# Moving weight conversions, normalising steps, folds and feature sums between the slots of a hand-planned mLSTM, Fourier and MLP kernel

## The chip, the core and the metric

The kernel runs on one core of a Trainium2 chip. The metric is the device time of one execution in microseconds (us); the time of a kernel is the median of its runs. Five engines work side by side, each through its own queue in order: TensorE (PE, with its weight loads as PEld), VectorE (DVE), ScalarE (ACT), GpSimd (POOL) and SyncE (SP), which here issues the DMAs. [...]

## The reference

Batch 4, 8 heads, 768 tokens, 40 features a head, all in float32. An mLSTM cell runs over the tokens of each head:

```python
m_new = np.maximum(f_gate[t] + m, i_gate[t])
f_stab, i_stab = np.exp(f_gate[t] + m - m_new), np.exp(i_gate[t] - m_new)
C = f_stab * C + i_stab * outer(v[t], k[t])        # 40 x 40 state
n = f_stab * n + i_stab * k[t]
y[t] = sigmoid(o_gate[t]) * (C @ q[t]) / max(abs(n @ q[t]), 1)
```

The eight heads of a token side by side are its 320 features x. Over them goes a Fourier mix and an MLP:

```python
u = x + real(fft(fft(x, axis=tokens), axis=features))
un = (u - mean(u)) / sqrt(var(u) + 1e-6)
out = u + relu(un @ w_ch1) @ w_ch2                 # 320 -> 1280 -> 320
```

## The kernel before

**A planner written out by hand.** Nothing is issued where it is defined. `at(slot, phase, fn, ...)` puts a step down, and `run` issues all steps in the order of (slot, phase). The phases are `EVAC` 0, `FILL` 1, `MAIN` 2, `FILL_PE` 3, with fractions between. A slot is about one step of the MLP on TensorE, which stands at `MAIN`; what stands at `FILL` comes before it on each queue, what stands at `FILL_PE` after it. Slot and phase thus set the order on each engine's queue and nothing else. Two steps that share no engine may change places without effect.

**The mLSTM.** Each batch's tokens are cut into six chunks c of 128. Batch 0 has a plan of its own; batches b of 1 to 3 go through `plan_halves`, three slots a chunk, beside the MLP of the batch before. For chunk (b, c), beginning in slot s:

- `mlstm_exp` (L491, ACT), `mlstm_scale_q` (L501, POOL) and `mlstm_mask` (L515, POOL) prepare weights and queries.
- `halves_scores` and `halves_to_state` (PE, `ps<-qk` and `ps<-vw`) write the scores' bank, which exists once. `halves_weigh` (L672, DVE) and two `halves_add` (L667, DVE, the state adds) read it, and free it for the next chunk.
- The heads: `halves_from_state` and the first `halves_from_chunk` (PE, `ph<-C,qg` and `ph<-kvt,W`), then `halves_between`, an ACT copy of one element (L699, `warm`) for which the second `halves_from_chunk` waits. Their bank exists once too.
- `mlstm_finish` (L712 to L720, five DVE instructions, the finish (b, c)) normalises and gates out of the heads' bank, and so frees it for the next chunk's heads. `halves_rows` (SP, some POOL) moves rows of chunks 0, 1, 2 and 3.

**The mix.** `mix_fold` (L812 to L828, mostly DVE) folds a pair of chunks for the transform; `mix_seq`, `mix_tail` and `mix_feat` (PE, `pz`, `pzt`, `pu`) transform; `mix_add` (L957 to L963, six DVE instructions, the addition of chunk c) adds the result and takes mean and variance; `mix_center` (L971), `mix_turn` and `mix_turn_out` (L983) turn the chunk. `mix_rstd` and three `mix_rstd_step` (L1002 to L1005, POOL) give the deviation by Newton steps.

**The MLP.** Batch 0's (slots 31 to 62) is plain: `mlp_in` (L1056 and L1047), `mlp_relu` (L1071), `mlp_out` (L1181), `residual` (L1187, DVE). Batches 1, 2 and 3 (32 slots each from 63, 95 and 127) save products by sums: `mlp_sums` (L1106, DVE, the feature sums) before the first block; five blocks of four slots (L1118, and L1123 for the tails), whose partial results DVE adds (L1127, one add in a block's second slot and three in its third); then three pairs of four slots each (L1237), each with two banks that TensorE overwrites in the next slot once DVE's residual (L1187) has read them, and `hidden_sums` (L1223, DVE).

**Weight conversions.** The MLP's weights come as 64-bit floats. Ten pieces are each loaded (SP, `raw`, two buffers), taken apart (`take`, L406 and L408, DVE), converted (`convert`, L413 and L414, ACT) and put together (`join`, L420, L422 and L426, DVE). Those of `w_ch2` are done beside batch 0's MLP; the list `when` holds slot and phase of each. Matmul results rotate over four banks given out by `bank`, and the mix of batches 2 and 3 has banks of its own choice among them.

Of the kernel before, what the change touches and what calls it, by code (L numbers as in the profile page):

```python
# [20 lines left out]
NT = S // L  # L21
# [9 lines left out]
TG = NT // 2  # L31
# [22 lines left out]
def kernel(  # L54
# [69 lines left out]
    def at(slot, phase, fn, *args):  # L124
        plan.setdefault((slot, phase), []).append((fn, args))
# [7 lines left out]
    EVAC, FILL, MAIN, FILL_PE = range(4)  # L133
# [628 lines left out]
    def plan_halves(b, s0, stride=3):  # L762
        for c in range(NT):
            s = s0 + stride * c
            t = 22 + 2 * c if b == 1 and c < 3 else s - 5
            at(t, FILL, mlstm_load, b, c)
            at(t, FILL, mlstm_load_max, b, c)
            at(34 if b == 1 and c == 2 else t + 1, FILL, mlstm_load_decay, b, c)
            at(s - 1, FILL, mlstm_load_o, b, c)
            at(s - 1, FILL, mlstm_scale_v, b, c)  # L770
            at(s - 1, FILL + 0.3, mlstm_exp, b, c, 0)
            at(s, FILL, mlstm_exp, b, c, NP)
            at(s, FILL_PE + 2.05, halves_scores, b, c)
            at(s, FILL_PE + 2.5, halves_to_state, b, c)
            for i in range(2):
                at(s + i, FILL + 0.05, halves_decay, b, c, i)
                at(s + 1 + i, FILL - 0.2, halves_add, b, c, i)
            at(s, FILL + 0.1, mlstm_scale_q, b, c)
            at(s + 1, FILL, mlstm_mask, b, c)
            at(s + 1, FILL + 0.55 if b == 1 and c > 0 else MAIN + 0.7, halves_weigh, b, c)  # L780
            end = c == NT - 1
            at(s + 3, MAIN - 0.1 if end else FILL_PE, halves_from_state, b, c)
            at(s + 3, MAIN - 0.1 if end else FILL_PE, halves_from_chunk, b, c, 0)
            at(s + 3, MAIN if end else FILL_PE + 0.5, halves_between, b, c)
            at(s + 3, FILL_PE + 3, halves_from_chunk, b, c, 1)
            at(s + 3, FILL_PE + 0.6, mlstm_tanh, b, c)
            at(s + (5 if (b, c) == (2, 2) else 4), FILL + 0.3 if b == 1 else MAIN + 0.55, mlstm_finish, b, c)
            at(s + 6, FILL - 0.6, halves_rows, b, c)

# [215 lines left out]
    def plan_mix(b, s0, x_done, s_feat, s_add, s_turn):  # L1007
        for j in range(TG):
            p = TG - 1 - j
            at(x_done[j] + (b > 1 and j == TG - 1), FILL + 0.5 if b < 2 else FILL_PE + 0.2, mix_fold, b, p)  # L1010
            if b == 0:
                at((s0 - 4, s0 - 2, s0)[j], FILL_PE + 4, mix_seq, b, p, (0, 1))
                at((s0 - 2, s0 - 2, s0)[j], FILL_PE + 4, mix_tail, b, p)
            elif b == 1 or j == 0:
                if b > 1:
                    for step, slot in enumerate((x_done[0], x_done[-1] + 2, x_done[-1] + 6)):
                        at(slot, FILL_PE + 0.25, mix_fold_again, b, step)
                at(s0, FILL_PE + 4, mix_seq, b, p, (0,))
                at(s0 + 1, FILL_PE + 4, mix_seq, b, p, (1,))
                at(s0 + 2, FILL_PE + 4, mix_tail, b, p)  # L1020
        for i in range(2):
            at(s0 + 1 if b == 0 else s0 + 1 + i, FILL, mix_seq_out, b, i)
        at(s0 + (1 if b == 0 else 3), FILL + 0.1, mix_tail_out, b)
        for p in range(TG):
            at(s_feat[p], FILL_PE + 4, mix_feat, b, p)
        for c, a, t in zip(ORDER, s_add, s_turn):
            at(a, FILL if b < 2 else MAIN + 0.5, mix_add, b, c)
            at(t, FILL + 0.1, mix_center, b, c)
            at(t, FILL_PE + (5 if b == 0 or c in ORDER[:4] else -0.1), mix_turn, b, c)
            if b > 0:  # L1030
                at(t, FILL_PE + 6, mix_turn_out, b, c)
            elif t < s_mlp:
                at(t + 1, FILL + 0.2, mix_turn_out, b, c)
            else:
                at(t + 1, EVAC, mix_turn_out, b, c)
# [232 lines left out]
    def plan_mlp(b, s):  # L1268
        groups = range(NT // TG)
        for i in range(NFF // 2) if b > 0 else ():  # L1270
            for step in range(4):
                at(s, MAIN, mlp_block, b, i, step)
                s += 1
            end = i == NFF // 2 - 1
            for n, (gr, f) in enumerate(((1, 2 * i + 1), (1, 2 * i), (0, 2 * i))):
                at(*((s - 1, MAIN + (-0.1 if gr else 0.1)) if end else (s + n, MAIN + 0.5)), mlp_relu_in_place, gr, f)
        for gr in groups if b == 0 else ():
            for f in range(NFF):
                at(s, MAIN, mlp_in, b, gr, f)
                s += 1  # L1280
                if f % 2:
                    at(s, EVAC, mlp_relu, b, gr, f - 1)
                    at(s, EVAC, mlp_relu, b, gr, f)
        if b > 0:
            for j in range(1, 5):
                at(s - (5, 4, 3, 3)[j - 1], FILL_PE + 0.3, hidden_sums, 0, (j,), 0, NFF // 2 - 2)
            at(s, EVAC, hidden_sums, 0, (1, 2), NFF // 2 - 2, NFF // 2)
            at(s, MAIN + 0.1, hidden_sums, 0, (3, 4), NFF // 2 - 2, NFF // 2)
        for n in range(TG) if b > 0 else ():
            for step in range(4):  # L1290
                at(s, MAIN, mlp_out_pair, b, n, step)
                if n < TG - 1 and step > 1:
                    for j in (2 * step - 3, 2 * step - 2):
                        at(s, MAIN + 0.6, hidden_sums, n + 1, (j,))
                s += 1
        for gr in groups if b == 0 else ():
            for i in range(TG):
                for half in range(2):
                    at(s, MAIN, mlp_out, b, gr, i, half)
                    s += 1  # L1300
                at(s, EVAC, mlp_store, b, gr, i)
# [5 lines left out]

    def plan_batch(b, s_mlstm, s_mix, s_mlp):
        (plan_halves if b > 0 else plan_mlstm)(b, s_mlstm)
        done = [s_mlstm + n for n in ((16, 19, 22) if b == 0 else (18, 21, 22))]  # L1310
        assert s_mix >= done[-1] and s_mlp >= s_mix + 9
        late = [s_mlp + 2 * c for c in range(TG)]
        if b == 0:
            feat = [s_mix + 1, s_mix + 1, s_mlp + 3]
            turn = [s_mix + 2, s_mix + 3, s_mix + 4]
            add = turn + [s_mlp, s_mlp + 4, s_mlp + 5]
            late = [s_mlp + 2, s_mlp + 5, s_mlp + 7]
        else:
            feat = [s_mix + c for c in ((3, 4, 6) if b == 1 else (3, 4, 7))]
            add = [s_mix + c for c in ((4, 4, 5, 6, 7, 7) if b == 1 else (4, 5, 5, 6, 8, 9))]  # L1320
            turn = [s_mix + c for c in ((5, 6, 6) if b == 1 else (6, 7, 8))]
            late = [s_mix + c for c in ((7, 8, 8) if b == 1 else (9, 10, 10))]
            at(s_mlp, EVAC + 0.5, mlp_sums)
        plan_mix(b, s_mix, done, feat, add, turn + late)
        s = s_mlp + NFF + 2
        at(s, FILL + 0.6, mix_rstd, b)
        for n in range(3):
            at(s + 3 * n if b == 0 else s, FILL + 0.65, mix_rstd_step, b)
        plan_mlp(b, s_mlp)

    s_mlp = 31
    plan_batch(0, 0, 22, s_mlp)
    plan_batch(1, 32, 54, s_mlp + MLP_SLOTS)
    plan_batch(2, 53, 83, s_mlp + 2 * MLP_SLOTS)
    plan_batch(3, 83, 115, s_mlp + 3 * MLP_SLOTS)
    for n in range(4):
# [4 lines left out]

    when = [((2, 0.7), (4, 0.5), (6, 0.6)), ((6, 0.7), (7, 0.5), (8, 0.6)), ((11, 0.7), (13, 0.5), (22, 0.6))]
    when += [((22, 0.7), (23, 0.7), (27, 0.6)), ((27, 0.7), (28, 0.7), (32, 0.6))]
    when += [((33, 0.7), (34, 0.3), (34, 0.6)), ((34, 0.7), (35, 2.7), (36, 0.6))]
    when += [((s, 0.7), (s + 1, 0.7), (s + 2, 0.6)) for s in (36, 39, 42)]
    pieces = w1_pieces + w2_pieces
    for n, (w, p) in enumerate(zip(when, pieces)):
        if n > 4:
# [138 lines left out]
```

## Time and profile before

| | |
|---|---|
| median of 14 runs | 402.73 us (401.38 to 403.95) |
| the profiled execution | 402.7 us, its span 401.0 us |
| TensorE busy | 382.9 us, 95% of the span |
| VectorE, ScalarE, GpSimd busy | 279.7, 171.8, 133.0 us |
| mean granted TensorE clock | 0.991 of full speed |
| DMA | 44.78 MB, 112 GB/s in the mean |

Times in the text that name no duration are microseconds from the span's start. In the timeline a row has the start, the length, engine, line, operation, tiles, shapes and count; in brackets the idle time of the engine before it and what ended that. Ends of matmuls are modelled, and pipelined matmuls start a little before their predecessor's end.

### The profile page before, as it was taken

How to read it: one execution, taken by the hardware profiler on the slowest of the kernel's cores; microseconds unless marked ns; L12 is line 12 of the kernel's file. 1: busy time of each engine (PE TensorE's matmuls, PEld its weight loads, DVE VectorE, ACT ScalarE, POOL GpSimd, SP SyncE). 2: the span in 40 equal slices, each digit the busy share in tenths (PEclk: the TensorE clock that was granted, in tenths of full speed). 3: DMA queues.
4: the chain of work that ended last, by engine and by line, in shares of the span. 5: the costliest groups of instructions: out<-in, count | busy, mean ns of one | idle time of the engine just before them, and what ended most of it. 6: DMA issues, size and time to landing. Idle time of an engine off the chain costs nothing.

```text
span 401.0 us, 10588 instructions
## 1 busy us (share of the span) xinstructions
PE 382.9 (95%) x4174; PEld 278.7 (69%) x4174; DVE 279.7 (70%) x671; ACT 171.8 (43%) x481; POOL 133.0 (33%) x237
## 2 busy tenths in 40 slices
PE   8999899979999999998999989989999999999996
PEld 6877555545567677755569888845578987556996
DVE  7789988999766467485775498777764686336652
ACT  6887367655640232655463214544440023454000
POOL 5648512555763341253255124451310000020000
PEclk9999999979999999999999999999999999999999
DMA  7988499777276244356800526410000000000000
GB/s 215 292 244 238 139 246 272 192 196 221 68 188 170 61 154 129 120 129 177 194 1 28 141 67 207 133 38 2 0 0 18 17 34 33 2 0 0 34 33 34
DMA packets 25631, 44.78 MB, mean 112 GB/s; under 512 B 5727, under 2 KB 14766, under 8 KB 25454
## 3 DMA queue, kind: packets, MB, share of 16 engines
q1 hardware_dynamic: 25582, 44.11, 38.4%
q8 instruction: 33, 0.54, 0.6%
q14 instruction: 16, 0.13, 0.1%
HBM read 38.49 MB, written 4.12 MB: 106 GB/s over the span
## 4 chain that ended last, share of the span: by engine, by line
PE 67%; DVE 22%; issue 5%; DMA 3%; ACT 2%; POOL 0%; SPq 0%; DVEq 0%; POOLq 0%
PE po L1237 18%; PE pm L1118 14%; PE po L1181 8%; PE pm L1056 5%; PE ph L519 4%; PE pm L1123 4%; PE ps L519 2%; PE pu L935 2%; DVE so L716 2%; DVE h L1127 2%; DMA qk<-in_qkT 1%; PE pz L892 1%; PE put L978 1%; DVE x L720 1%; PE pm L1047 1%
## 5 line engine op out<-in xcount | busy, mean ns | idle before, releaser
L1187 DVE SCALAR_TENSOR_TENSOR x<-po,rstd,x 128x160 f32<-128x160 f32 (+1 forms) x69 | 26.9, 394 | 43.7 <-PE po L1237 36.8
L1127 DVE TENSOR_TENSOR h<-h,pm 128x384 f32<-128x384 f32 x60 | 30.5, 549 | 29.2 <-PE pm L1123 13.9
L652 POOL TENSOR_TENSOR C<-C,decB 128x164 f32<-128x164 f32 x30 | 15.9, 531 | 75.8 <-DVE C L667 66.4
L1118 PE MATMUL pm<-uT,w_sb 128*128 128x384 f32 x90 | 37.8, 507 | 2.0 <-DVE h L1127 1.3
L491 ACT ACTIVATE W<-W,colT 128x64 f32<-128x64 f32 x144 | 37.3, 339 | 0.0
L1181 PE MATMUL po<-w_sb,h 128*128 128x320 f32 x120 | 34.2, 435 | 0.0
L515 POOL TENSOR_SCALAR_AFFINE_SELECT W<-W 64x512 f32<-64x512 f32 x36 | 27.5, 764 | 12.3 <-ACT W L491 11.1
L1056 PE MATMUL pm<-uT,w_sb 128*128 128x384 f32 x80 | 31.2, 528 | 0.3 <-DVE x L955 0.2
L1002 POOL TENSOR_TENSOR t<-rstd 128x6 f32<-128x6 f32 x12 | 3.4, 282 | 81.9 <-DVE v L996 81.3
L1237 PE MATMUL po<-T,S 128*128 128x160 f32 x180 | 27.9, 302 | 1.5 <-DVE x L1187 1.5
L501 POOL TENSOR_TENSOR qg<-qk,Gb 128x512 f32<-128x512 f32 (+1 forms) x21 | 28.8, 1370 | 0.8 <-DMA Gb<-G_d 0.7
L1181 PEld LDWEIGHTS po<-w_sb,h 128*128 128x128 f32 x120 | 22.3, 190 | 9.4 <-issue 0.6
L1237 PEld LDWEIGHTS po<-T,S 128*128 128x128 f32 x180 | 25.5, 190 | 3.2 <-DVE x L1187 2.0
L1118 PEld LDWEIGHTS pm<-uT,w_sb 128*128 128x128 f32 x90 | 15.5, 189 | 16.3 <-DVE h L1127 7.5
L1237 PE MATMUL po<-w_sb,h 128*128 128x160 f32 x180 | 26.3, 300 | 0.0
L1237 PEld LDWEIGHTS po<-w_sb,h 128*128 128x128 f32 x180 | 25.2, 190 | 1.4 <-DVE x L1187 0.3
L1174 ACT ACTIVATE h<-h 128x384 f32<-128x384 f32 x45 | 23.1, 520 | 2.0 <-DVE h L1127 2.0
L1123 PE MATMUL pm<-uT,w1t_sb 64*128 64x384 f32 x120 | 23.4, 509 | 0.0
L983 ACT COPY uT<-put 128x384 f32<-128x384 f32 x24 | 11.1, 476 | 27.5 <-PE put L978 27.5
L1056 PEld LDWEIGHTS pm<-uT,w_sb 128*128 128x128 f32 x80 | 15.1, 202 | 11.0 <-issue 3.2
L971 ACT ACTIVATE uc<-x 128x384 f32<-128x384 f32 x24 | 14.4, 613 | 18.3 <-DVE x L963 12.2
L507 POOL TENSOR_TENSOR vw<-kvt,colT 128x328 f32<-128x328 f32 x23 | 17.8, 772 | 12.8 <-DVE colT L360 10.1
(241 smaller groups left out, 843.6 us busy)
## 6 DMA issues: line engine op xcount, KB each, us to landing
kvt<-in_kv SPq DMA_DIRECT2D x24, 336.0 KB
qk<-in_qkT SPq DMA_DIRECT2D x48, 160.0 KB
raw<-in_w SPq DMA_DIRECT2D x10, 640.0 KB
Gb<-G_d SPq DMA_DIRECT2D x36, 128.0 KB
W<-M_d SPq DMA_DIRECT2D x36, 128.0 KB
so<-in_o SPq DMA_DIRECT2D x24, 160.0 KB
out<-x SPq DMA_DIRECT2D x24, 160.0 KB
x<-so SPq DMA_DIRECT2D x9, 140.0 KB
```

The costliest lines, as they stand in the source:

```text
L491: nc.scalar.activation(out=k.W[:, h, :], in_=M, func=AF.Exp, scale=-1.0, bias=colT[:, c, 0, b * H + h:b * H + h + 1])
L501: nc.gpsimd.tensor_tensor(out=k.qg[:, :, t], in0=k.qk[:, 0, :, t], in1=k.Gb[:, :, t], op=OP.mult)
L515: nc.gpsimd.affine_select(out=W, in_=W, compare_op=OP.is_ge, fill=0.0, base=base, pattern=[[0, H], [step, LH]], channel_multiplier=-1)
L519: nc.tensor.matmul(out, w, x, start=start, stop=True, skip_group_check=True)
L1056: nc.tensor.matmul(k.pm[i], w1_sb[:, ch, f0:f0 + L], u[2 * ch], start=(ch == 0 and not ahead), stop=(ch == 1 and ahead), skip_group_check= ...
L1118: nc.tensor.matmul(bank, w, u, start=start, stop=True, skip_group_check=True)
L1123: nc.tensor.matmul(bank, block(w1t_sb, i)[rows], mlp_u(gr, 1)[rows], start=False, stop=True, skip_group_check=True)
L1127: nc.vector.tensor_tensor(out=h, in0=h, in1=bank, op=OP.add)
L1174: nc.scalar.activation(out=h, in_=h, func=AF.Relu, scale=-1.0)
L1181: nc.tensor.matmul(k.po, hidden(gr, f)[:, i * L:(i + 1) * L], w2_sb[:, f, :], start=(f == 0), stop=(f == NFF - 1))
L1187: nc.vector.scalar_tensor_tensor(out=u, in0=po, scalar=k.rstd[:, c:c + 1], in1=u, op0=OP.mult, op1=OP.add)
L1237: nc.tensor.matmul(po, a[:, f], w[:, f], start=start and f == 0, stop=f == half - 1, skip_group_check=True)
```

## The change

No instruction is added or taken away; steps get another slot or phase.

- Weight pieces 6 to 9 (counted from 0): the convert goes behind the slot's state adds and exponentials, the join one slot later or at the slot's head, and take and load of pieces 7 to 9 a slot later.
- Folds of batch 1: from slots 50, 53 and 54 to 49, 50 and 52.
- Finishes: (2,5) two slots later; (3,0) and (3,2) one slot later; (2,4), (3,3) and (3,4) in their slot, but ahead of the MLP step's adds.
- Heads of (2,5): in their slot 71, but behind the MLP step and no longer ahead of it.
- `halves_rows` is not called for chunks 4 and 5, for which it does nothing.
- Batches 2 and 3: the addition of chunk 5 goes one slot earlier, into the slot of chunk 0's (87 and 119).
- Feature sums of batches 2 and 3: from the head of the first block's slot to the end of the slot before.

```diff
-            end = c == NT - 1
+            end = c == NT - 1 and b != 2
...
-            at(s + (5 if (b, c) == (2, 2) else 4), FILL + 0.3 if b == 1 else MAIN + 0.55, mlstm_finish, b, c)
-            at(s + 6, FILL - 0.6, halves_rows, b, c)
+            at(s + ((4, 4, 4, 4, 4, 4), (4, 4, 5, 4, 4, 6), (5, 4, 5, 4, 4, 4))[b - 1][c],
+               FILL + 0.3 if b == 1 or (b, c) in ((2, 4), (3, 3), (3, 4)) else MAIN + 0.55, mlstm_finish, b, c)
+            if c < TG + 1:
+                at(s + 6, FILL - 0.6, halves_rows, b, c)
...
-        done = [s_mlstm + n for n in ((16, 19, 22) if b == 0 else (18, 21, 22))]
+        done = [s_mlstm + n for n in ((16, 19, 22), (17, 18, 20), (18, 21, 22), (18, 21, 22))[b]]
...
-            add = [s_mix + c for c in ((4, 4, 5, 6, 7, 7) if b == 1 else (4, 5, 5, 6, 8, 9))]
+            add = [s_mix + c for c in ((4, 4, 5, 6, 7, 7) if b == 1 else (4, 4, 5, 6, 8, 9))]
...
-            at(s_mlp, EVAC + 0.5, mlp_sums)
+            at(*((s_mlp, EVAC + 0.5) if b == 1 else (s_mlp - 1, MAIN + 0.7)), mlp_sums)
...
-    when += [((33, 0.7), (34, 0.3), (34, 0.6)), ((34, 0.7), (35, 2.7), (36, 0.6))]
-    when += [((s, 0.7), (s + 1, 0.7), (s + 2, 0.6)) for s in (36, 39, 42)]
+    when += [((33, 0.7), (34, 0.3), (34, 0.6)), ((34, 0.7), (36, 0.7), (37, 0.3))]
+    when += [((s, 0.7), (s + 2, 0.7), (s + 3, 0.3)) for s in (37, 40, 43)]
```

## Prediction

> **What bounds the kernel now.** I read the page first, then TensorE's own waits, then the sums by stretch and the timeline around each wait.
>
> ```profile
> span 401.0 us, 10588 instructions
> ...
> PE 382.9 (95%) x4174; PEld 278.7 (69%) x4174; DVE 279.7 (70%) x671; ACT 171.8 (43%) x481; POOL 133.0 (33%) x237
> ```
>
> Who TensorE waited for (us in total, times, longest us):
>
> ```profile
> PE po L1237 <- DVE x L1187: 2.5, 3, 1.1
> PE ps L519 <- DVE C L667: 1.9, 1, 1.9
> PE ph L519 <- ACT warm L699: 1.4, 2, 1.1
> PE pm L1118 <- DVE h L1127: 1.3, 2, 1.0
> ...
> PE ph L519 <- DVE x L720: 1.0, 1, 1.0
> ```
>
> The sums by stretch (length, then busy PE, PEld, DVE, ACT, POOL, then granted clock, DMA share, GB/s):
>
> ```profile
> 82.00:87.00 5.00, 1.99 (x95) 1.65 (x86) 4.70 (x6) 3.33 (x9) 2.93 (x3) 0.77 0.71 212
> 87.00:91.50 4.50, 4.50 (x13) 2.72 (x10) 3.88 (x10) 2.19 (x7) 2.82 (x4) 0.50 0.89 252
> 91.50:95.00 3.50, 3.50 (x13) 1.55 (x11) 3.24 (x5) 3.13 (x8) 2.27 (x2) 1.00 0.94 280
> ```
>
> TensorE is the bound: it idles 401.0 - 382.9 = 18.1 us. Since the change leaves its work alone, only these waits can move, plus one stretch at half clock: the last rows show 0.77, then 0.50, then 1.00. The timeline (start, length, what, wait before it) shows why:
>
> ```profile
> 77.68 2.82 PE L1056 MATMUL pm<-uT,w_sb 128*128 128x384 f32 x8 [0.16 <-DVE x L955]
> ...
> 80.42 0.81 DVE L420 SCALAR_TENSOR_TENSOR e<-raw,e 128x640 uint32<-128x640 uint32 x1
> ...
> 83.39 0.83 ACT L413 ACTIVATE e<-e,ebias 128x640 uint32<-128x640 uint32 x1 [3.65 <-DVE e L406]
> 83.67 0.32 DVE L667 TENSOR_TENSOR C<-C,ps 128x164 f32<-128x164 f32 x1
> 84.04 0.69 PE L519 MATMUL ps<-qk 40*64 40x64 f32 x32 [1.86 <-DVE C L667]
> ...
> 86.40 0.67 PE L519 MATMUL ph<-kvt,W 64*64 64x41 f32 x16 [1.15 <-ACT warm L699]
> ...
> 87.69 4.63 PE L1056 MATMUL pm<-uT,w_sb 128*128 128x384 f32 x8
> ...
> 201.81 0.91 PE L1118 MATMUL pm<-uT,w_sb 128*128 128x384 f32 x2 [0.22 <-DVE h L1127]
> ```
>
> A weight join (L420) and take stand ahead of the short state add (L667) that frees the scores' bank; on ACT the convert (L413), waiting for that take, stands ahead of the copy (L699) that TensorE waits for next. Then eight passes take 4.63 us instead of 2.82.
>
> **Weight conversions.** The join and the next take go behind the second state add, the convert behind the exponentials and the copy. Gone: 1.86 + 1.15 = 3.0 us of waits; 0.4 of pipelining, since a successor otherwise starts about 0.2 us before its predecessor's modelled end; 4.63 - 2.82 = 1.8 at half clock; and 0.35 on the transposes behind (0.90 instead of 0.55 at 76.97). Sum 5.6.
>
> Next late: the last join moves to slot 46. It fits DVE's 2.74 us wait before the state add at 112.18 if it runs like the join at 80.42 (0.81 + 0.81 + 0.83 = 2.5), not if like the one at 84.25 beside POOL (to 88.2, 4.0). The finish of chunk 4 follows, and the next heads start at 114.99, only 0.4 us after its end at 114.61. Cost 0 to 1.6; I take 0.5, nearer the first join, since only one large POOL step (L501, 111.14 to 112.42) lies there. First part: -5.1. On ACT one convert now lies ahead of the copy L983 at 77.55 and delays it by 0.75 us; it frees a bank at 78.8 that the third matmul of the 77.68 group, two pairs of passes on, wants at 79.0. Nothing, or up to 0.75 if that cover goes. On SP, raw loads stand behind row moves instead of ahead; raw is loaded two slots ahead and the one wait for it on DVE was 1.64 at 67.61, behind which nothing of TensorE was late. Nothing.
>
> **Feature sums, rows, folds of batch 1.** `mlp_sums` keeps its neighbours on every queue except for the finish dealt with below, and rows of chunks 4 and 5 issue nothing: both free. The folds (1.7 us each) and POOL's third Newton step move before the first residual at 123.66, for which DVE waited 2.79. Free; without that cover one residual is 0.5 late, against four rotating banks.
>
> **Finishes (2,4), (2,5) and the heads behind the block.** Finish (2,4) (1.65 us, 187.10 to 188.75) runs in the 2.49 us that DVE waits before 185.70; the 1.02 at 188.89 goes. Heads (2,5) lose their cover: a block's pair of passes lay between their first half and the half that waits for the ACT copy. Now the pair comes first (187.7), the first half at 188.35 for 0.95, the copy 0.1 behind it for 0.13, the second half from 189.6 for 0.4: slot 72 starts at 190.0 instead of 190.99. But finish (2,5), 1.65 us now placed in a 1.72 us wait, goes to slot 74, into a stretch without a gap: from the end of slot 73's adds (196.19) to those of slot 77 (201.22) DVE works 5.0 us; then 6.7, from 1.0 earlier, so the adds come at 201.9 and TensorE restarts 0.6 later than today: its wait there grows from 0.22 to 1.8. Bounds -1.0 (DVE catches up) to +1.0. I take +0.6.
>
> **Two additions share slot 87, finish (3,0) to slot 88.** The addition (1.74 us) and the finish (1.71) change places ahead of the residual that TensorE waits 1.08 for at 234.88: no change. But the finish then ends at 238.4, and the heads at 237.80 need its bank: a wait of 0.75 (with the 0.14 that followed L720 at 188.75), in front of all that TensorE has queued, of which 0.44 is recovered at 247.28, where TensorE waits for DVE anyway. +0.3 (0 to 0.8).
>
> **Finish (3,2) to slot 94, (3,3) ahead of an add.** (3,2) would start at the residual after 257.35 and end at 259.4 (today 257.39). Heads at 258.57 wait 1.0; the feature sums start at 259.3 instead of 258.44. Finish (3,3) (1.65) delays the add at 263.24, whose bank the tails then overwrite. The wait of 1.04 at 266.70 takes some of that in. Bounds: 0 (today's sums, 4.2 us beside POOL, run like those at 336.87, 2.3) to 0.9; I take +0.5.
>
> [...]
>
> **Batch 3, same pair of additions in slot 119.** Today both stand in slot 120, and TensorE waits 1.01 at 321.55. One goes ahead of a residual that frees a bank at 317.33: new wait 0.5, old one gone. -0.6 (-1.0 to 0).
>
> **Sum.** -5.1 + 0.6 + 0.3 + 0.5 - 0.6 = -4.3. The profiled execution took 402.7 us (span 401.0 and 1.7 around it), the runs' median being 402.73: 398.4 us.
>
> **Rivals.** (a) The half clock stays in the first MLP for another reason: 1.8 + 0.35 less, 400.6. Against: nowhere else did it fall, and it fell inside the stretch with the only wait above 1.3. [...]
>
> (b) Slower: the half clock moves to the new waits. It lasted from about 84.7 (the 0.77 above) to 91.5, 6.8 us; among dense matmuls that costs 3.4. New places: the 1.8 us at 200.6 to 202.4, and the 1.0 before the small heads at 258.57. One gives 401.8, two give 405.2; two decide. For: 1.8 is the size that did it. Against: four waits of 1.0 to 1.1 (188.89, 234.88, 266.70, 321.55) cost no clock, and matmuls around 201 are dense.
>
> (c) Transfers become the bound of the first MLP. From 82 to 95 they moved 5 x 212 + 4.5 x 252 + 3.5 x 280 thousand bytes, 3.2 MB; in 13 - 5.6 = 7.4 us that is 430 GB/s, against 292 in the best slice. At that rate they take 10.9 us and come 3.5 late, less their lead in the buffers (0 to half): 400.1 to 401.9. Against: the 10 us behind them moved only 68 GB/s.
>
> **Chances.** Forecast 0.60, (a) 0.12, (b) once 0.10, twice 0.05, (c) 0.10, below the range 0.03. The range goes down by two thirds of what all small terms at their lower ends would give (0.5 + 1.6 + 0.3 + 0.5 + 0.4 = 3.3), to 396.2, and up to 401.2, which takes in (a) and most of (c). About 0.2% (0.8 us) can be told from no change: faster 0.87 (all but part of (b), with 401.8 on the edge), same 0.05, slower 0.08.
>
> **What would show it.** Right: no wait at `ps<-qk` and `warm` near 82 to 87, clock 1.00 there, the second x8 group at 2.8; a wait near 1.8 on L1127 in the fourth block of batch 1; waits on L720 at the heads of (3,1) and (3,3); none at the T4 product of batch 3's second pair. Wrong: a half clock anywhere, or waits for DMA or L667 in slots 41 to 50.

## The result: 407.86 us, 1.3% slower, and the profile after

The median after is 407.86 us (10 runs, 406.49 to 408.76), against 402.49 for the kernel before on the same chip. The ratio is 1.0135, with a 95% interval of 1.0119 to 1.0150: 5.4 us slower, where 4.3 us faster was forecast. The profiled execution took 408.68 us, 5.98 more than the one before. From the page after, the span and the busy times:

```profile
span 406.9 us, 10596 instructions
...
PE 387.4 (95%) x4174; PEld 280.8 (69%) x4174; DVE 280.9 (69%) x671; ACT 171.9 (42%) x481; POOL 133.8 (33%) x237
```

TensorE idles 406.9 - 387.4 = 19.5 us, only 1.4 more than before. Its busy time grew by 4.5 us for the same 4174 matmuls: it ran slower for longer, at a mean granted clock of 0.983 instead of 0.991. Who TensorE waited for (us in total, times, longest us):

```profile
PE ph L519 <- DVE x L720: 3.4, 3, 1.7
PE pm L1125 <- DVE h L1129: 2.1, 2, 1.7
PE ph L519 <- DVE so L720: 1.6, 2, 0.8
PE po L1239 <- DVE x L1189: 1.3, 2, 1.1
```

The waits of 1.86 and 1.15 us in the first block are gone, as forecast. In their place stand waits for the last instruction of the finishes (L720) and one of 1.7 us before the tails (L1125). The sums by stretch of the kernel after (columns as in the prediction; the granted clock is the third number from the end):

```profile
82.00:95.00 13.00, 13.00 (x192) 7.55 (x183) 12.51 (x21) 8.17 (x21) 9.64 (x11) 1.00 0.88 252
95.00:112.00 17.00, 13.70 (x283) 8.57 (x283) 13.19 (x30) 8.80 (x29) 11.62 (x21) 1.00 0.47 118
114.20:117.60 3.40, 3.40 (x23) 1.86 (x23) 2.69 (x9) 1.53 (x6) 3.09 (x9) 0.50 0.95 236
...
264.40:267.80 3.40, 1.68 (x8) 0.79 (x8) 2.88 (x8) 1.51 (x6) 1.17 (x3) 1.00 0.02 7
267.80:278.00 10.20, 10.20 (x125) 6.15 (x123) 3.85 (x11) 1.94 (x5) 2.95 (x4) 0.50 0.06 18
278.10:281.50 3.40, 3.40 (x58) 1.86 (x58) 0.55 (x1) 1.24 (x4) 0.00 (x0) 1.00 0.00 0
```

From 82 to 95 TensorE has no gap, at full clock, where it was busy 9.99 of 13 us at a mean clock of 0.74 before. But from 95 to 112 it is now idle for 3.3 us (before, 0.0 of the same 17), and two stretches run at half clock, one of them 10.2 us long.

Where the 6 us went is seen when each matmul of the one trace is set against the same matmul of the other, which gives TensorE's lead (by how much a matmul starts earlier than the same one before) by stretch:

| stretch (before) | lead of the kernel after at its start and end, us | loss | forecast |
|---|---|---|---|
| up to 80 us | 0 to 0.9 (not of the change: most traces here lie between 1 ahead and 0.7 behind by this point, one 3.6 behind) | -0.9 | |
| first block, 80 to 95 | 0.9 to 6.9 | -6.0 | -5.6 |
| first block, 95 to 120 | 6.9 to 0.8 | +6.1 | +0.5 |
| finishes (2,4), (2,5), 184 to 204 | 0.8 to 0.2 | +0.6 | +0.6 |
| slots 87 and 88, 234 to 252 | 0.2 to 0.0 | +0.2 | +0.3 |
| finish (3,2), 256 to 260 | 0.0 to -1.0 | +1.0 | +0.5 for this row and the next |
| sums, finish (3,3), clock, 260 to 275 | -1.0 to -6.6 | +5.6 | |
| batch 3's additions, 316 to 324 | -6.6 to -5.9 | -0.7 | -0.6 |

Four of the six terms came out within 0.5 us. Two did not: what the first block gives back, and what the finishes of batch 3 cost.

### The profile page after: what moved, and what is told of

Same layout as the page of the kernel before. It is cut to its first block, busy times and chain, and to the rows that moved or that the text cites. A ratio compares the mean times of both kernels' runs of the same rounds, so it can differ in the third digit from the quotient of the medians.

```text
span 406.9 us, 10596 instructions
## 1 busy us (share of the span) xinstructions
PE 387.4 (95%) x4174; PEld 280.8 (69%) x4174; DVE 280.9 (69%) x671; ACT 171.9 (42%) x481; POOL 133.8 (33%) x237
## 4 chain that ended last, share of the span: by engine, by line
PE 70%; DVE 19%; issue 3%; ACT 3%; DMA 2%; POOL 2%; SPq 0%; DVEq 0%; POOLq 0%; ACTq 0%
PE po L1239 19%; PE pm L1120 16%; PE po L1183 8%; PE pm L1125 4%; PE ph L519 3%; PE pu L937 3%; PE ps L519 2%; DVE w_sb L426 2%; DVE so L716 2%; PE put L980 2%; DMA raw<-in_w 1%; PE pz L906 1%; PE pz L894 1%; DVE m L422 1%; DVE stats L964 1%
## 5 line engine op out<-in xcount | busy, mean ns | idle before, releaser
L652 POOL TENSOR_TENSOR C<-C,decB 128x164 f32<-128x164 f32 x30 | 17.3, 576 | 71.7 <-DVE C L667 56.0
L515 POOL TENSOR_SCALAR_AFFINE_SELECT W<-W 64x512 f32<-64x512 f32 x36 | 27.3, 759 | 13.1 <-ACT W L491 11.9
L1004 POOL TENSOR_TENSOR t<-rstd 128x6 f32<-128x6 f32 x12 | 3.5, 292 | 84.8 <-DVE v L998 84.3
L1125 PE MATMUL pm<-uT,w1t_sb 64*128 64x384 f32 x120 | 25.9, 516 | 2.1 <-DVE h L1129 2.1
L1120 PEld LDWEIGHTS pm<-uT,w_sb 128*128 128x128 f32 x90 | 16.3, 198 | 16.2 <-DVE h L1129 7.2
L1125 PEld LDWEIGHTS pm<-uT,w1t_sb 64*128 64x128 f32 x120 | 12.4, 186 | 14.0 <-issue 8.2
L507 POOL TENSOR_TENSOR vw<-kvt,colT 128x328 f32<-128x328 f32 x23 | 17.5, 761 | 12.4 <-DMA qk<-in_qkT 10.1
```

The lines of the kernel that those rows point to most:

```text
L515: nc.gpsimd.affine_select(out=W, in_=W, compare_op=OP.is_ge, fill=0.0, base=base, pattern=[[0, H], [step, LH]], channel_multiplier=-1)
L1120: nc.tensor.matmul(bank, w, u, start=start, stop=True, skip_group_check=True)
L1125: nc.tensor.matmul(bank, block(w1t_sb, i)[rows], mlp_u(gr, 1)[rows], start=False, stop=True, skip_group_check=True)
```

## Experiments on the parts

How long the clock is halved differs from one execution of a kernel to the next: by the clocks of its runs, the kernel after spent 6.5 to 13.8 us at half clock (mean 10.3), the kernel before about 6.

**The conversions alone**, the kernel before with only this part:

```diff
-    when += [((33, 0.7), (34, 0.3), (34, 0.6)), ((34, 0.7), (35, 2.7), (36, 0.6))]
-    when += [((s, 0.7), (s + 1, 0.7), (s + 2, 0.6)) for s in (36, 39, 42)]
+    when += [((33, 0.7), (34, 0.3), (34, 0.6)), ((34, 0.7), (36, 0.7), (37, 0.3))]
+    when += [((s, 0.7), (s + 2, 0.7), (s + 3, 0.3)) for s in (37, 40, 43)]
```

> The kernel before with the weight conversions' new slots and nothing else. Theory 1 (the gain was made and given back: in the trace after, TensorE is 6.0 us ahead of the trace before at 100 us and 0.1 us ahead at 120 us, because VectorE's finishes of batch 1 come late behind joins and takes): within 1 us of before, so 401.5 to 403.5. Rival, the forecast's own reading (the conversions are worth 5.1 us and another part of the change eats them): 396.5 to 398.5.

403.88 us, ratio 1.0025 (1.0002 to 1.0048), 0.4 above the range of theory 1 and far from the rival's. In its trace the lead goes from 1.0 to 7.0 us and is back at 0.8 by 118 us, with the same four waits as in the kernel after. The gain was real and was given back whole, by this part itself.

**After without the conversions** (the same diff backwards):

> The kernel after with the weight conversions back in their old slots. Theory 1: what the change costs lies in the other parts, so this stays within 1 us of after, 407 to 409. Rival, the forecast's reading: after without its best part, 412 to 413. A third way: the conversions' part is the culprit, and this falls to 402 to 404.

404.25 us (1.0027 to 1.0064 of before): neither of the first two cases, and just above the third range. The change without its best-looking part is 3.6 us faster than with it, though that part alone costs only 1.0. The parts do not add up.

**Batch 3's finishes and the sums alone**:

```diff
+            at(s + (5 if (b, c) in ((2, 2), (3, 2)) else 4),
+               FILL + 0.3 if b == 1 or (b, c) in ((3, 3), (3, 4)) else MAIN + 0.55, mlstm_finish, b, c)
...
+            at(*((s_mlp, EVAC + 0.5) if b == 1 else (s_mlp - 1, MAIN + 0.7)), mlp_sums)
```

> The kernel before with only the finishes of chunks 2, 3 and 4 of batch 3 and the feature sums of batches 2 and 3 moved. Theory 1 (these moves put waits of 0.9 and 1.7 us among the small matmuls at 258 to 267 us, and a stretch of half clock over dense matmuls follows): 406 to 408.5, with a half clock behind the wait before the tails in some or all runs. Rival (the waits alone, 0.5 as forecast to 1.6 as the trace after shows them): 403 to 404.1, with no half clock there.

404.24 us (1.0019 to 1.0059), so about 1.5 us, as the rival has it; before the tails TensorE waits 1.03 us, and no half clock follows.

**After without these** (the same lines backwards):

> The kernel after with those finishes and sums back in their places. Theory 1: 401.5 to 403.5, no half clock near 268 us. Rival (waits alone): 406.3 to 407.4.

402.80 us (0.9982 to 1.0034). On top of the rest they cost 5.1 us; alone, 1.5.

**Two pieces alone**: finish (2,4) ahead of the adds, and the two additions in one slot for batch 3 only.

```diff
-            at(s + (5 if (b, c) == (2, 2) else 4), FILL + 0.3 if b == 1 else MAIN + 0.55, mlstm_finish, b, c)
+            at(s + (5 if (b, c) == (2, 2) else 4), FILL + 0.3 if b == 1 or (b, c) == (2, 4) else MAIN + 0.55,
+               mlstm_finish, b, c)
...
-(4, 5, 5, 6, 8, 9)
+(4, 4 if b == 3 else 5, 5, 6, 8, 9)
```

> The kernel before with two pieces of the change alone: the finish of chunk 4 of batch 2 ahead of the additions (no other finish moved), and two transform additions in one slot for batch 3 only. The prediction's terms: -1.0 for the wait at 188.89 and -0.6 for the additions; the trace after shows about -1.0 and -0.75. Theory: 400.8 to 401.3. Rival (both come back at the next wait for VectorE): within 0.4 us of before.

400.64 us, ratio 0.9952 (0.9932 to 0.9971). Both terms hold, -1.1 and -0.7 in the trace.

## Experiments on the first block: who took the gain back

These are the rows of the kernel after, by the timeline:

```profile
99.59 0.16 DVE L998 TENSOR_SCALAR v<-v 128x6 f32<-128x6 f32 x1
99.76 0.44 POOL L1004 TENSOR_TENSOR t<-rstd 128x6 f32<-128x6 f32 x1 [4.60 <-DVE v L998]
...
102.08 0.45 POOL L652 TENSOR_TENSOR C<-C,decB 128x164 f32<-128x164 f32 x1
102.56 0.32 DVE L667 TENSOR_TENSOR C<-C,ps 128x164 f32<-128x164 f32 x1 [2.01 <-POOL C L652]
...
104.74 0.49 DVE L720 TENSOR_TENSOR so<-ph,so 128x320 f32<-128x320 f32 x1
105.38 0.68 PE L519 MATMUL ph<-C,qg 40*64 40x41 f32 x32 [0.81 <-DVE so L720]
...
106.42 0.78 POOL L1004 TENSOR_TENSOR t<-rstd 128x6 f32<-128x6 f32 x1
...
109.57 0.32 DVE L667 TENSOR_TENSOR C<-C,ps 128x164 f32<-128x164 f32 x1 [0.83 <-POOL C L652]
...
111.78 0.77 PE L519 MATMUL ph<-C,qg 40*64 40x41 f32 x32 [1.68 <-DVE x L720]
```

Read from the bottom of each group. TensorE waits for a finish (L720). The finish stands behind a state add (L667), which waits for the state decay (L652) on GpSimd. That stands in GpSimd's queue behind a Newton step of batch 0's deviations (four instructions from L1004). The Newton step waited 4.60 us for VectorE's part (L998), which stands behind a weight join. The same chain is in the trace before, where nobody on TensorE waited for it:

```profile
101.78 0.78 POOL L1002 TENSOR_TENSOR t<-rstd 128x6 f32<-128x6 f32 x1 [3.08 <-DVE v L996]
...
105.82 0.33 DVE L667 TENSOR_TENSOR C<-C,ps 128x164 f32<-128x164 f32 x1 [1.72 <-POOL C L652]
```

The finish behind that add ended at 108.49 before and at 105.23 after (L720: 104.74 + 0.49), 3.3 us earlier, while TensorE was 6 us earlier. The finishes before and behind it came 3.5 and 3.0 us earlier (ending at 96.03 instead of 99.58, and at 111.63 instead of 114.61). In the trace before, the heads that need their bank started 2.6, 2.0 and 0.4 us behind these three ends. That slack and the earlier ends together allow these heads leads of 6.2, 5.3 and 3.4 us at most. Measured are 6.0, 5.1 and 3.2.

**Deviations of batch 0 later**, on the kernel with the conversions alone:

```diff
-        s = s_mlp + NFF + 2
+        s = s_mlp + NFF + (2 if b else 7)
...
-            at(s + 3 * n if b == 0 else s, FILL + 0.65, mix_rstd_step, b)
+            at(s + 1 + n if b == 0 else s, FILL + 0.65, mix_rstd_step, b)
```

> The kernel before with the conversions' new slots, and the inverse deviations of batch 0 five slots later (slot 48, its three GpSimd steps in slots 49 to 51). Theory: in slots 43 to 47 a join delays VectorE's part of them, the GpSimd steps wait for that at the head of GpSimd's queue, and the state decays, additions, finishes and heads behind them come late; so the waits of 0.81 and 1.68 us before the heads of chunks 3 and 4 of batch 1 shrink by 1.5 to 2.5 us together: 400 to 402.5, with TensorE 1.5 to 2.5 us ahead of the kernel before at 125 us. Rival (VectorE's conversions alone are too long for the stretch): those waits stay within 0.3 us and the time is that of the conversions alone, 403 to 404.5.

400.75 us, ratio 0.9963 (0.9942 to 0.9984), by the medians 3.1 less than the conversions alone (2.5 by the ratios to before). The trace keeps 2.4 us of the lead. The wait at the heads of chunk 3 fell from 0.81 to 0.24; that at those of chunk 4 did not shrink (1.88): ahead of it now stood the last join, 3.6 us beside GpSimd.

**Only the two conversions that stood ahead of the old waits**:

```diff
+    when += [((37, 0.7), (38, 0.7), (39, 0.3)), ((39, 0.7), (40, 0.7), (41, 0.6)), ((42, 0.7), (43, 0.7), (44, 0.6))]
```

> The kernel before with only the two conversions moved whose join and convert stood ahead of the two waits at 82 and 85 us; the last two stay in their old slots. Theory (the time given back is given back because the last joins moved into slots 40 to 46): the gain at 95 us is still 5 to 6 us, less than half of it is lost by 125 us, 398 to 400.5. Rival (whatever is gained early is lost until VectorE and GpSimd, whose work has not moved, catch up): within 1 us of before.

403.46 us (0.9990 to 1.0034). This tells nothing of the theories: the convert of slot 38, ahead of the copy `warm` again, waited 3.38 us for its take, and TensorE 3.87 us for the copy, so that there was no lead at 95 us to lose.

**The last join behind the finish of chunk 4 too** (and the deviations one more slot later; the loop of the change is written out here):

```diff
-(43, 0.7), (45, 0.7), (46, 0.3)
+(43, 0.7), (45, 0.7), (48, 0.6)
```

> The kernel before with the conversions' new slots, the inverse deviations of batch 0 later (slot 49, GpSimd steps in slots 50 to 52), and the last join behind the finish of chunk 4 of batch 1 (slot 48 instead of 46). Theory (in the kernel with the deviations alone moved, that join, 3.6 us beside GpSimd, stands ahead of the addition and finish for which TensorE waits 1.88 us at 110 us): that wait goes, about 399 against 400.8. Rival (the additions wait for GpSimd's decays in any case): the wait stays above 1.2 us and the time within 0.7 us of 400.8.

398.64 us, ratio 0.9893 (0.9871 to 0.9916). The 1.88 is gone. The same two stretches of this kernel, for comparison with the kernel after:

```profile
82.00:95.00 13.00, 13.00 (x292) 8.33 (x291) 12.65 (x18) 7.60 (x21) 10.24 (x10) 1.00 0.83 230
95.00:112.00 17.00, 15.90 (x326) 10.04 (x325) 15.26 (x31) 10.51 (x33) 11.10 (x14) 1.00 0.49 131
```

TensorE idles 1.1 us from 95 to 112 instead of 3.3, and all six runs have a mean clock of 1.000. The conversions' part is thus worth 4.4 us, near the 5.1 of the forecast, once two steps make room for it: the deviations, and the last join, which the change itself had moved from slot 44 to 46. In its trace, waits of 0.85 and 0.25 us before heads are left.

**The take of the last piece but one behind the finish of chunk 2 as well**, its convert and join later, and the last piece's take and convert behind these:

```diff
-((40, 0.7), (42, 0.7), (43, 0.3)), ((43, 0.7), (45, 0.7), (48, 0.6))
+((42, 0.6), (43, 0.7), (45, 0.6)), ((45, 0.7), (46, 0.7), (48, 0.6))
```

> As the one with the last join moved, and the take of the fourth-last conversion step (for the last but one piece) behind the finish of chunk 2 too, with its convert and join one and two slots later. Theory: the 0.8 us before the heads of chunk 2 goes as well, about 398. Rival (the work only moves on to the finish of chunk 3 or 4): a wait of the same size comes there, 399 to 400.

398.80 us (0.9874 to 0.9928): no better. The 0.85 at the heads of chunk 2 turned into waits of 0.58 and 0.72 for the copy `warm` there and at chunk 3, a form of the rival.

## Experiments on batch 3: the wait, the clock and one place in VectorE's stream

**Only finish (3,3) back behind the add**, on the kernel after:

```diff
-(b, c) in ((2, 4), (3, 3), (3, 4))
+(b, c) in ((2, 4), (3, 4))
```

> The kernel after with only the finish of chunk 3 of batch 3 put back behind the addition that frees the tails' bank. Theory (the 1.72 us wait before the tails brings the half clock behind it): that wait falls to 1.1 or less, no half clock near 268 us, 403 to 404.5. Rival (any late piece of that stretch, the finish of chunk 2 and the sums, does it): the half clock stays and the time is above 406.5.

405.15 us (1.0037 to 1.0083), 2.7 less than after and between the two cases. The wait of 1.7 us did not fall, it moved: 1.68 us, from 266.12, before the product behind the tails. There was no half clock near 268 in the profiled execution. What the finish costs and what the clock costs are not told apart by this run.

**The wait filled with work**: the same waits for VectorE, but TensorE multiplies meanwhile.

```diff
+            if b == 2 and i == 0:
+                for n in range(2):
+                    product(p3, block(w1x["S4"], i), mlp_u(1, 2), True)
             tails(1, (p3, p5))
```

> The kernel after with two more copies of a product (128x384, about 0.8 us each, the same bank written again with the same values) in front of the tails, in the place of the 1.72 us wait at 265 us: the same waits for VectorE, TensorE not idle. Theory (idle time trips the clock, and the half clock is most of the loss there): no half clock near 268 us, 403.5 to 405.5. Rival (the waits themselves are the loss, and the clock follows something else): 407.3 to 408.6, with the half clock still there.

404.87 us (1.0038 to 1.0091 of before). The two groups of sums of this kernel:

```profile
264.00:267.60 3.60, 3.15 (x11) 1.41 (x10) 3.04 (x9) 2.41 (x10) 2.02 (x3) 1.00 0.18 50
268.00:278.00 10.00, 10.00 (x188) 6.01 (x184) 4.89 (x14) 4.04 (x11) 2.96 (x4) 1.00 0.07 18
```

TensorE is busy 3.15 of 3.60 us, the clock behind it stays at 1.00 where it was 0.50, and the kernel is 3.0 us faster for two products more. In its trace TensorE loses 1.8 us between 256 and 275 (by the times of the trace before) where the kernel after loses 6.6. Most of what the idle time cost, it cost through the clock.

**Conversions and batch 3's finishes with the sums, nothing else**:

> The kernel before with the conversions' new slots and the moves of batch 3's finishes and sums, nothing else. Alone the one costs 1.0 us and the other 1.4 to 1.6. Theory (the two together lengthen the wait before the tails to 1.7 us, which brings the half clock there; one alone leaves it at 1.0): 406 to 407.5, with two or more half-clock stretches of 3.4 us in most runs. Rival (they only add up, and the other parts of the change trip the clock): 404.5 to 405.5, one or two stretches.

404.14 us (1.0019 to 1.0067): 0.4 below the rival's range, and far from the theory's. Before the tails the wait is 1.03 us, with no half clock there. So a third thing made it 1.7. A second trace of the kernel after:

> The kernel after once more, for a second trace. Theory: waits of 1.7 us before the tails near 265 us again and a half clock behind it, at another moment of its 3.4 us steps. Rival (the wait of 1.7 is a chance of one execution): 1.0 us as in the kernels without the conversions' new slots, and no half clock.

408.20 us: the wait is 1.72 us again, followed by 10.24 us at half clock. So the wait belongs to the program and is no accident of one execution. Set side by side, the finish (3,3) of the traces differs in one instruction only. The kernel after, then the kernel with two fills more, from the next experiment (whose line numbers are 3 higher):

```profile
265.10 0.90 DVE L716 SCALAR_TENSOR_TENSOR so<-so,den 128x320 f32<-128x320 f32 x1 [0.46 <-ACT h L1161]
...
267.04 2.20 PE L1125 MATMUL pm<-uT,w1t_sb 64*128 64x384 f32 x6 [1.72 <-DVE h L1129]
```

```profile
264.38 0.56 DVE L719 SCALAR_TENSOR_TENSOR so<-so,den 128x320 f32<-128x320 f32 x1
...
265.99 1.23 PE L1128 MATMUL pm<-uT,w1t_sb 64*128 64x384 f32 x5 [1.03 <-DVE h L1132]
```

The instruction starts 0.46 us behind its predecessor instead of 0.10 and takes 0.90 instead of 0.56; by then GpSimd's `vw` (L507) runs, which began 0.18 us earlier. The named releaser, an ACT copy, is nothing that this instruction needs: in the kernel without the conversions the same instruction starts at 265.00, before that copy ends (265.24). Count VectorE's records (instructions and semaphore waits) from the start, the first as number 0. Then the late one is number 575 in every trace with the 1.7 us wait and the same order of finish and add, and in the kernel with the two products, where VectorE is late all the same; with 1.03 us it is number 570, 571 or 574. In some other traces one such step of the first block is late by as much (0.46 to 0.48), and there it is number 191. Both are one less than a multiple of 64, and 384 = 3 x 128 apart.

**The place shifted away and onto it**, by fills of unused columns at VectorE's start, two in the kernel after and four in the kernel with conversions, finishes and sums:

```diff
         nc.vector.memset(ebias, -896.0 * 2.0**23)
+        for n in range(2):
+            nc.vector.memset(spare[:, n:n + 1], 0.0)
```

> The kernel after with two more fills of one unused column each on VectorE at the very start, so that every later instruction of VectorE stands two places further on in its record. In the kernels with the 1.72 us wait before the tails, the normalising step of chunk 3 of batch 3 is VectorE's record number 575 (nine times 64, less one), behind a semaphore record, and starts 0.46 us late; the same step is number 570, 571 or 574 in those with 1.03 us, and starts 0.10 late. Theory (each 64th place costs VectorE 0.4 us where no work hides it): the step is number 577, starts 0.10 late, the wait falls to 1.0 to 1.1 us, no half clock near 268 us, and the time falls by about 3, to 404 to 405.5. Rival (something else of that combination delays the step): wait of 1.7 us, half clock and 407.3 to 408.6 as before.

> The kernel with the conversions' new slots and batch 3's finishes and sums alone, with four such fills: the same step moves from place 571 to 575. Theory: it starts 0.46 us late, the wait before the tails grows from 1.03 to 1.7 us, the half clock comes near 268 us in most runs, and the time rises from 404.1 by 2 to 3.5 us. Rival: no change, 403.8 to 404.6.

Two fills more make the kernel after 403.54 us (ratio to before 1.0025, 1.0008 to 1.0042), 4.3 less. Four fills make the other 407.75 us (1.0123, 1.0095 to 1.0150), 3.6 more. The step and the clock of the kernel with four:

```profile
263.33 0.90 DVE L719 SCALAR_TENSOR_TENSOR so<-so,den 128x320 f32<-128x320 f32 x1 [0.46 <-ACT h L1163]
```

```profile
262.50:265.90 3.40, 1.67 (x7) 0.78 (x7) 2.88 (x7) 1.64 (x6) 1.31 (x3) 1.00 0.01 2
266.00:276.20 10.20, 10.20 (x125) 6.07 (x123) 3.89 (x11) 1.94 (x5) 2.95 (x4) 0.50 0.06 18
```

Both theories held in the waits (1.03 and 1.73 us) and in the clock; the times moved a little more than forecast. Fills that do no work thus take the loss away in one kernel and bring it in another. This settles why the parts did not add up: the other edits change how many semaphore records stand ahead of the finish (3,3) (VectorE has 152 of them in the kernel after and 143 in the one before, with 671 instructions in both), and in the kernel after one of its instructions falls on a place that costs 0.4 us.

**After with the first block mended** (deviations and last join as above):

> The kernel after with only the first block's mends: deviations of batch 0 in slots 49 to 52 and the last join in slot 48. On the kernel with the conversions alone these were worth 5.2 us. Theory (what was given back in the first block and the clock near 268 us are separate losses): 403 to 404.5, the half clock at 268 us still there in most runs. Rival (the clock there goes with what happens in the first block): 401 to 402, no half clock.

401.38 us, ratio 0.9972 (0.9945 to 0.9999), 6.5 less than after. The step is number 575 again, the wait 1.73, and 3.4 us of half clock follow in the trace (and 3.4 more at 79 us, behind a wait of 2.0 at the transposes; the trace of the kernel after has neither there); by their clocks, 4 of 12 runs had no half clock at all. The time is near the rival's, the trace shows what the theory said: the losses are separate, but the second one is smaller here, and why the half clock lasts 3.4 us in one kernel and 10.2 in another stays open.

**The best version** joins the mended conversions and the two good pieces:

> Both together: conversions, deviations, last join and take as in the second of this set, and the two pieces as in the third. Theory (the gains lie in different stretches and add up): about 396.5. Rival: no better than the better half of it, 398 or more.

> The last join and deviations moved as before, with the two good pieces of the change (finish of chunk 4 of batch 2, additions of batch 3). Theory (they add up): 398.6 - 2.0 = 396.6, and no half clock. Rival: not under 397.5, as with the take moved too.

With the take moved too, 397.58 us (0.9842 to 0.9889), between its two cases; without it, as the theory has it, 396.45 us, ratio 0.9852 (0.9827 to 0.9877): 6 us faster than the kernel before and 11 than the kernel after, with a mean clock of 1.000 in its five runs.

## Why the prediction was wrong, point by point

**Weight conversions: the step that failed is "Next late ... I take 0.5".** The gains were right: no wait at `ps<-qk` or `warm`, full clock, 6.0 us gained by 95 us against 5.6. What is late next was looked for in one place only, the last join against the last wait before a state add, and 0.5 us was put on it. Measured is 6.1: 0.9 at the finish of chunk 2, 1.0 at chunk 3, 1.8 at chunk 4, and 2.3 behind those, in a wait of 0.57 for a late mask (L515, GpSimd) and a half clock of 3.4 us. The list of TensorE's waits cannot show this, because before the change TensorE came 6 us later and found these steps done, by 2.6, 2.0 and 0.4 us. The prediction checked the third of these slacks alone, and with the old times of the steps. The row that did show it was VectorE's own wait of 1.72 us for GpSimd's decay at 105.82. Moving TensorE 6 us forward asked whether decay, add and finish could come 6 us earlier too; they came 3.3 earlier. Two steps held those of chunks 3 and 4: the deviations, which the change does not touch, and the last join, which it put two slots later. The experiments on the two show it; the 0.85 at chunk 2 stayed.

**Finishes (2,4) and (2,5), slots 87 and 88, batch 3's additions: right in size**, with +0.6, +0.2 and -0.7 for +0.6, +0.3 and -0.6. The waits came where they were said to come: 0.77 before the heads at 237.69, 0.91 at 258.64, 0.24 left before the T4 product. For (2,4) and (2,5) the sum is in part luck, as both halves were 0.5 too large: 0.5 us gained by slot 72 (a wait of 0.32 for the copy `warm` was left) for 1.0, then 1.1 lost for 1.6. The wait near 201 was split into 0.38 and 0.50 in place of 1.8.

**Finish (3,2) and (3,3): the bound of 0.9 failed.** The term was +0.5 at most 0.9; measured are 1.1 us (from 0.4 us ahead to 0.8 behind in the kernel after with two more fills), and 5.5 on top of it in the trace where the finish falls on place 575 (4.3 by the medians of the two kernels). Of these 5.5, 10.24 us at half clock make about 5.1 (an estimate: half their length, as TensorE is busy all through). The upper bound of 0.9 is nearer to the 1.1 than the 0.5 taken: the sums behind (3,2) took 4.6 us from start to end where they took 4.2 before, and did not run like those at 336.87 (2.3). The waits were seen; the place and the clock behind it were not.

**Rival (b) is half of what happened.** The half clock moved to a new wait among the heads and tails of batch 3; the prediction named the wait at 258.57, 7 us earlier, and priced a half clock at 3.4 us. Its chance of 0.15 rested on four waits of 1.0 to 1.1 us without a half clock, which still holds: here it took 1.7. The other half is the loss in the first block, and the forecast's range left out the sum of the two. Rival (a) did not hold by itself: in the first block a half clock did stay, but behind new waits, at 114 us. Rival (c) did not hold: at 252 GB/s from 82 to 95, TensorE waited for no transfer there.

**A wait as the cause of the half clock: right.** In the first block the clock is 1.00 from 82 to 95 with the waits of 1.86 and 1.15 us gone (0.74 before), and the half clock at 267.81 stands behind a wait of 1.72 us and goes when that wait is filled (1.00 from 268 to 278).

## What to carry to other kernels

A wait that is taken away moves everything behind it forward: before counting the gain, follow each chain that the next stages need (here decay, add, finish) through the other engines' own waits, since steps that end just in time show no wait on the bound engine. Put steps with slack (here deviations and the last join) out of such a chain first, and then the gain stays. And where a small edit moves the time by several us at another place, look at the granted clock and at where single instructions of a stream start late, before believing in the edit's logic.

## What the runs showed of the hardware

**The clock changed in steps of 3.41 us, and was halved behind steps in which TensorE was little busy.** All stretches at half clock last 3.41 us or a multiple (6.83 from 84.66 before; 3.41 from 114.21 and 10.24 from 267.81 in the kernel after), but for those at the end of an execution, which end with its trace. Within a trace they start on one grid: 114.21 and 267.81 in the kernel after lie 45 steps of 3.413 apart. In each of the 16 falls ahead of a kernel's last 3.4 us the step just before held 1.18 to 1.86 us of busy TensorE (1.68 of 3.40 in the row from 264.40). Over the 19 traces whose grid a fall gives, every step at full clock with less than 1.6 us was followed by a fall, and none with 2.03 or more. In between six were and seven were not (1.60 to 1.81), so there the busy time alone does not decide. So steps with about half their time idle, in one gap or several, were followed by half clock; behind a gap of 1.03 us, in the kernel after with two more fills, the clock stayed at 1.00. The wait of 1.68 us in the kernel with only finish (3,3) back was followed by no fall: on that trace's grid (from its fall at 403.42) a step ends at 266.89, inside the wait, and the steps on both sides held 2.64 and 2.50 us. The grid does not lie at the same place in each execution of a kernel: the second trace of the kernel after is at half clock from 267.00 to 277.20, the first at full clock until 267.81. That the scatter of one kernel's runs comes from this is not shown.

**At two places of VectorE's stream an instruction started 0.4 us late.** This was counted on the instruction `so<-so,den` of the finishes, where it stands behind a semaphore record. At places 191 and 575 it started 0.40 to 0.42 us behind that record in all of 9 cases (0.42 at 191 in the kernel before, 0.40 at 575 in the kernel after); at 357 other places, 0.04 to 0.18. But at place 255, one less than a multiple of 64 as well, it started 0.04 us behind it in all of 3 cases, so the 64 of the expectations does not hold; a step of 128 fits these places, and so would one of 384. An instruction can thus start late, and its engine wait, though nothing that it reads is late. The page lists DMA packets of the kind `instruction`, 16 of them with 0.13 MB on queue q14 in the kernel after, 8 KB each. In all 20 traces one of these starts within 3.0 us of each of VectorE's places 63, 191, 319, 447 and 575, and none within 3.9 us of 127, 255, 383, 511, 639 and 767. What makes the instruction late at 191 and 575 is not shown.

**A small GpSimd instruction took up to 4 times as long beside VectorE.** The first instruction of a Newton step (128x6) took 0.20 us alone at 109.68 in the trace before, and 0.78 beside a join at 101.78; the four of a step together took 1.1 and 2.7 us from start to end.
